# PSUM as two score strips and four single banks, with score pieces issued in twos

## The chip, the cores and the metric

The kernel runs on one core of one Trainium2 chip. The metric is the device time in microseconds (us); a median over several executions is quoted. The trace of one execution covers a span that is 1.6 to 1.9 us shorter than its time, so times are compared with times and spans with spans.

## The reference

Eight batches of eight-head causal attention (576 tokens, head size 64, and 16 "beacon" keys and values that every token may see), followed by an MLP with a squared ReLU over all 4608 tokens.

```python
B, H, S, Nb, D = (8, 8, 576, 16, 64)
k_all = np.concatenate([beacon_k, k], axis=2)
v_all = np.concatenate([beacon_v, v], axis=2)
scores = scale * np.matmul(q, k_all.transpose(0, 1, 3, 2))   # causal mask on the last S keys
a = np.exp(scores - scores.max(-1, keepdims=True))
a /= a.sum(-1, keepdims=True) + 1e-09
x = np.matmul(a, v_all)             # -> (4608, 512)
h = x @ w_in                        # 512 -> 2048
r = np.maximum(h, 0.0)
out = (r * r) @ w_out               # 2048 -> 512
```

## The kernel before

The kernel is not written in the order in which it runs. Every piece of work is an operation with modelled durations, a priority and the buffers it takes; a list scheduler plays these through and then emits the instructions of each engine in the order found. So a change of a buffer pool changes the order on all engines.

PSUM is where TensorE puts its results. The kernel takes it as eight banks of 512 fp32 columns. Before, these are four tiles of two banks each, shared by everything:

```python
ps = [psum.tile([128, 2, 512], FP32, name=f"ps{i}") for i in range(4)]
order = Order(
    pools={"ps": range(4), "stg": range(NSTG), "pt": range(NPT)},
    limits={"strip": 2, "av": 2, "mlp": 2, "tp": 1},
)
```

A head pair's scores come in four pieces. One piece fills one tile: the two heads of the pair are two 64-row matmuls, on the upper and the lower half of the array at once (their starts are 3 ns apart in the trace), each into its own bank. One exp on ScalarE (ACT) empties the tile.

```python
for i, (mms, off, width) in enumerate(ph.pieces):
    def emit_qk(e, mms=mms, box=box):
        st = ps[box["qk"].held[2]]
        for c, t0, t1, at in mms:
            for hj in range(2):
                hp = slice(64 * hj, 64 * hj + 64)
                nc.tensor.matmul(st[:, hj, at:at + t1 - t0],
                                 kT[b % 2][hp, pr, 128 * c:128 * c + 128],
                                 qT[b % 2][hp, pr, t0:t1], start=True, stop=True)
    qk = add(..., "PE", 0.05 + cols / 2400.0, emit_qk, ..., take=("ps", "strip"), gate=gate)
    # one exp for each piece; then a mask, AV (both heads in one tile), normalise
```

The MLP's units are two 128-column tiles of w_in for 512 tokens (eight 512-column matmuls, 1.73 us of TensorE), emptied by one relu over 1024 columns. The last output is copied and stored per 128 tokens, but both copies wait for the last matmul of both:

```python
deps = [s2_ops[j, u]]          # the last matmul unit of the two-tile output
ev = add(f"ev{j}.{u}", "ACT", 1.05 if ts is None else 0.6, emit_ev, prio=-15.0, deps=deps, ...)
```

For the first three batches q and k are transposed on TensorE (96x64 tiles; the beacon keys 16x128); later batches are transposed by DMA.

The softmax here doesn't subtract the row's maximum and nothing guards it: scores larger than these inputs give would overflow.

Of the kernel before, what the change touches and what calls it, by code (L numbers as in the profile page):

```python
# [9 lines left out]
FP32 = mybir.dt.float32  # L10
# [6 lines left out]
class Op:  # L17
# [3 lines left out]
                 "take", "give", "gate", "held", "dma", "pe_time", "behind", "followers",  # L21
                 "sync", "insts")

    def __init__(self, name, engs, dur, emit, prio=0.0, deps=(), take=None, give=None,
                 gate=None, dma=0.0, pe_time=0.0, behind=(), sync=()):
        self.name = name
        self.engs = engs if isinstance(engs, (tuple, list)) else (engs,)
        self.dur = dur
        self.emit = emit
        self.prio = prio  # L30
        self.sync = list(sync)
        self.need = list(deps) + self.sync
        self.users = []
        self.take = take
        self.give = give
        self.gate = gate
        self.held = None
        self.dma = dma
        self.pe_time = pe_time
        self.behind = list(behind)  # L40
        self.followers = []


class Order:
# [18 lines left out]
    def run(self):  # L63
# [24 lines left out]
        while events:  # L88
            now = events[0][0]
            while events and events[0][0] <= now + 1e-9:  # L90
# [6 lines left out]
                elif kind == "give":  # L97
                    pool, cls, idx = op.give.held
                    self.pools[pool].append(idx)
                    if cls in self.inuse:  # L100
                        self.inuse[cls] -= 1
            again = True
            while again:
                again = False
                for e in engines:
# [4 lines left out]
                    for op in avail[e]:  # L110
                        if any(free[x] <= now + 1e-9 for x in op.engs[:op.engs.index(e)]):
                            continue
                        if op.take:
                            pool, cls = op.take
                            if not self.pools[pool]:
                                continue
                            if cls in self.limits and self.inuse[cls] >= self.limits[cls]:
# [21 lines left out]
                    if op.take:  # L139
                        pool, cls = op.take  # L140
                        op.held = (pool, cls, self.pools[pool].pop(0))
                        if cls in self.inuse:
                            self.inuse[cls] += 1
# [33 lines left out]
def kernel(  # L177
# [62 lines left out]
    rcp = [sb(f"rcp{i}", [128, 2, NT], FP32) for i in range(4)]  # L240
    tri = sb("tri", [128, 4, 128], BF16)
    ps = [psum.tile([128, 2, 512], FP32, name=f"ps{i}") for i in range(4)]

    def wait_for(later, first):
# [4 lines left out]
        pools={"ps": range(4), "stg": range(NSTG), "pt": range(NPT)},  # L249
        limits={"strip": 2, "av": 2, "mlp": 2, "tp": 1},  # L250
# [126 lines left out]
    def add_strided(b, prio):  # L377
# [17 lines left out]
        for pr in range(HP):  # L395
# [3 lines left out]
            def emit_tp(e, pr=pr, h=h, box=box):  # L399
                pp = ps[box["t"].held[2]].bitcast(BF16)  # L400
                nc.tensor.transpose(pp[:, 1, 0:Nb], bks[b % 2][:, h, :], ident[0:Nb, 0:Nb])
                for half, at, t in ((1, Nb, ks), (0, 0, qs)):
                    for u in range(NS):
                        for hj in range(2):
                            nc.tensor.transpose(pp[64 * hj:64 * hj + 64, half, at + u * NP:at + (u + 1) * NP],  # L405
                                                t[b % 2][:, 2 * pr + hj, u, :], ident[0:NP, 0:NP])

            busy = qk_ops[HP * (b - 2) + pr] if b >= 2 else []
            tp = add(f"tp{b}.{pr}", "PE", 0.8 if b else 1.3, emit_tp, prio=100.0 * (HP * b + pr) - 190,
                     deps=[bk, loads[pr, "k"], loads[pr, "q"], ident_op] + busy, take=("ps", "tp"))  # L410
            box["t"] = tp

            def emit_k(e, pr=pr, box=box):
                pp = ps[box["t"].held[2]].bitcast(BF16)
                copy_on(e, kT[b % 2][:, pr, 0:Nb], pp[:, 1, 0:Nb])
                copy_on(e, kT[b % 2][:, pr, Nb:Nb + S].rearrange("p (n s) -> p n s", s=NS),
                        pp[:, 1, Nb:Nb + S].rearrange("p (s n) -> p n s", s=NS))

            def emit_q(e, pr=pr, box=box):
                pp = ps[box["t"].held[2]].bitcast(BF16)  # L420
                copy_on(e, qT[b % 2][:, pr, 0:S].rearrange("p (n s) -> p n s", s=NS),
                        pp[:, 0, 0:S].rearrange("p (s n) -> p n s", s=NS))

            ek = add(f"ek{b}.{pr}", "DVE", 0.9, emit_k, prio=-200.0, deps=[tp])
            eq = add(f"eq{b}.{pr}", ("DVE", "ACT"), 0.75, emit_q, prio=-199.0, deps=[tp])
            add(f"tpg{b}.{pr}", "-", 0.0, None, prio=0.0, deps=[ek, eq], give=tp)
# [67 lines left out]
    def add_phase(b, pr, p, n, ph, take_pt, qk_deps, gate):  # L494
        base = 100.0 * p + 1000.0 * n
        exps = []
        for i, (mms, off, width) in enumerate(ph.pieces):
            cols = sum(max(96, t1 - t0) for _, t0, t1, _ in mms)
            box = {}

            def emit_qk(e, mms=mms, box=box):
                st = ps[box["qk"].held[2]]
                for c, t0, t1, at in mms:
                    for hj in range(2):
                        hp = slice(64 * hj, 64 * hj + 64)
                        nc.tensor.matmul(  # L506
                            st[:, hj, at:at + t1 - t0],
                            kT[b % 2][hp, pr, 128 * c:128 * c + 128],
                            qT[b % 2][hp, pr, t0:t1],
                            start=True, stop=True,  # L510
                        )

            qk = add(f"qk{p}.{n}.{i}", "PE", 0.05 + cols / 2400.0, emit_qk, prio=base + i,
                     deps=qk_deps + [take_pt], take=("ps", "strip"), gate=gate)
# [3 lines left out]
            def emit_exp(e, off=off, width=width, box=box):  # L518
                st = ps[box["qk"].held[2]]
                nc.scalar.activation(pt[take_pt.held[2]][:, :, off:off + width], st[:, :, 0:width],  # L520
                                     AF.Exp, bias=0.0, scale=scale)

            exps.append(add(f"exp{p}.{n}.{i}", "ACT", 0.18 + 2 * width / 1200.0, emit_exp, prio=base + i,
                            deps=[qk], give=qk))
# [16 lines left out]
        def emit_av(e):  # L541
            P = pt[take_pt.held[2]]
            a = ps[av.held[2]]
            for hj in range(2):
                h = 2 * pr + hj
                for t in tl:
                    for c in range(t + 1):
# [3 lines left out]
                            a[:, hj, (t - tl[0]) * (D + 1):(t - tl[0] + 1) * (D + 1)],  # L551
# [5 lines left out]
        av = add(f"av{p}.{n}", "PE", 0.07 + 0.064 * sum(t + 1 for t in tl), emit_av, prio=base - 150,  # L557
                 deps=[mask] + [cast[b, "v", c] for c in range(tl[-1] + 1)] + av_ops[p], take=("ps", "av"),
                 give=take_pt if ph is phases(b)[-1] else None)
        av_ops[p].append(av)  # L560

        def emit_norm(e):
            a = ps[av.held[2]][:, :, 0:nt * (D + 1)].rearrange("p h (t d) -> p h t d", d=D + 1)
            r = rcp[(2 * p + n) % len(rcp)][:, :, 0:nt]
            nc.vector.reciprocal(r, a[:, :, :, D])  # L565
            nc.vector.tensor_tensor(  # L566
                out=xn[b % 2].rearrange("p t (h d) -> p h t d", d=D)[:, 2 * pr:2 * pr + 2, tl[0]:tl[0] + nt],
                in0=a[:, :, :, 0:D],
                in1=r[:, :, :, None].to_broadcast([128, 2, nt, D]),
                op=ALU.mult,  # L570
            )

        deps = [av]
        if b >= 2:
            deps += [o for (bb, _), o in xt_ops.items() if bb == b - 2]
        norm_ops[p, n] = add(f"norm{p}.{n}", "DVE", 0.4 + 0.133 * nt, emit_norm, prio=base - 150, deps=deps, give=av)
# [5 lines left out]
    s2_first = {}  # L582
# [7 lines left out]
    def add_xt(b):  # L590
        for t in range(NT):
# [7 lines left out]
            deps = [norm_ops[HP * b + i, 0] for i in range(HP)] + ring_deps(tok, tok + n)  # L599
# [4 lines left out]
    def add_xt_pe(b):  # L604
        for k, ph in enumerate(phases(b)):
            for pr in range(HP):
# [3 lines left out]
                def emit_tp(e, pr=pr, box=box, ph=ph):  # L610
                    pp = ps[box["t"].held[2]].bitcast(BF16)
                    for t in ph.tiles:
                        n = t_rows(t)
                        nc.tensor.transpose(pp[:, 0, t_start(t):t_start(t) + n],
# [3 lines left out]
                         deps=[norm_ops[HP * b + pr, k]], take=("ps", "tp"))  # L618
                box["t"] = tp

                def emit_ev(e, pr=pr, box=box, lo=lo, hi=hi):
                    pp = ps[box["t"].held[2]].bitcast(BF16)
                    at = (b * S) % RING
                    copy_on(e, xT[:, pr, at + lo:at + hi], pp[:, 0, lo:hi])
# [28 lines left out]
    def add_chunk(j):  # L653
# [11 lines left out]
        for f in range(NFT // 2):  # L665
            sqs = []
            for n, (lo_, hi_) in enumerate(parts):
                spans = [(lo_, wrap), (wrap, hi_)] if lo_ < wrap < hi_ else [(lo_, hi_)]
                N = hi_ - lo_
                box = {}  # L670

                def emit_s1(e, f=f, spans=spans, box=box):
                    h = ps[box["s1"].held[2]]
                    for u in range(2):
                        ft = 2 * f + u
                        for lo, hi in spans:
                            for mc in range(NMC):
                                nc.tensor.matmul(h[:, u, lo - spans[0][0]:hi - spans[0][0]],  # L678
# [4 lines left out]
                s1 = add(f"s1.{j}.{f}.{n}", "PE", 1.73 * N / TCH, emit_s1, prio=base + f + 0.5 * n,  # L683
                         deps=feeds_of(lo_, hi_) + [w_ops["in", f // 2]]
                         + [s2_ops[j - 2, u] for u in range(2) if j >= 2],
                         take=("ps", "mlp"), pe_time=1.73 * N / TCH)
                box["s1"] = s1
                s1_ops[lo_, hi_].append(s1)

                def emit_relu(e, f=f, lo=lo_ - t0, hi=hi_ - t0, box=box):  # L690
                    h = ps[box["s1"].held[2]][:, :, 0:hi - lo]
                    dst = G[:, 2 * f:2 * f + 2, lo:hi]
                    if e == "ACT":
                        nc.scalar.activation(dst, h, AF.Relu, bias=0.0, scale=1.0)  # L694
                    else:
# [138 lines left out]
```

## Time and profile before

| | before |
|---|---|
| time, median of 4 | 355.49 us (354.92 to 356.18) |
| span of the trace | 353.2 us |
| TensorE busy | 334.7 us (95%) |
| first matmul, first MLP matmul | 4.2 us, 27.6 us |
| start of the last matmul to the end | 5.1 us |

The head of the page, and its row of the granted clock:

```profile
span 353.2 us, 7173 instructions
...
PE 334.7 (95%) x2943; PEld 178.6 (51%) x2980; DVE 148.9 (42%) x287; ACT 193.4 (55%) x233; POOL 85.5 (24%) x132
...
PEclk9999999999999999999999999999999999999999
```

PE is TensorE and PEld its weight loads, DVE is VectorE, POOL GpSimd. 2943 matmuls are recorded and the program has 2980: 37 records are missing.

The row of the clock reads 9 (90% or more) from the start, and there it misleads: the trace has no record of the clock before 24.3 us, and until then TensorE runs at half pace. Two runs of the same 24 AV matmuls, one on each side:

```profile
22.60 1.52 PE L550 MATMUL ps<-vb,pt 128*128 128x65 bf16 x24
24.77 0.89 PE L550 MATMUL ps<-vb,pt 128*128 128x65 bf16 x24
```

From start to start the median AV matmul takes 54 ns before 24.3 us and 29 ns after it, a pair of transposes 80 and 43 ns.

Next, who TensorE waited for after 27 us, from the list of waits (total us, times, longest):

```profile
PE ps L506 <- DMA kT<-qk_area: 1.0, 1, 1.0
PE ps L678 <- ACT qT L280: 0.6, 1, 0.6
PE ps L718 <- issue: 0.5, 3, 0.2
PE ps L718 <- DMA stg<-in_k_dram: 0.2, 1, 0.2
```

So TensorE almost never waits after the start, and still "busy" is not "useful". The timeline of TensorE shows why (columns: start, length, engine, line, operation, output<-inputs, shapes, count). L506 are scores, L718 and L678 the MLP, L550 attention output (AV):

```profile
179.64 0.38 PE L506 MATMUL ps<-qT,kT 64*128 64x496 bf16 x2
179.95 1.68 PE L718 MATMUL ps<-w_out,g 128*128 128x512 bf16 x7
181.78 0.55 PE L506 MATMUL ps<-qT,kT 64*128 64x464 bf16 x6
182.26 1.90 PE L718 MATMUL ps<-w_out,g 128*128 128x512 bf16 x8
184.10 0.30 PE L506 MATMUL ps<-qT,kT 64*128 64x208 bf16 x4
184.33 1.90 PE L718 MATMUL ps<-w_out,g 128*128 128x512 bf16 x8
186.07 1.91 PE L678 MATMUL ps<-xT,w_in 128*128 128x256 bf16 x16
```

Read starts, not lengths (the ends of matmuls are modelled). Between two runs without a score run (184.33 to 186.07) eight 512-column matmuls take 1.74 us, or 216 ns each. From 182.26 to 184.10 the same eight take 1.84: about 0.10 us more, because a score run follows. The score run of 184.10 has 208 + 80 columns, 0.12 us at 2400 columns per us (256 columns take 109 ns from start to start, 512 take 216), and the next run starts 0.23 us later: another 0.11. A score run between full-array work thus costs about 207 ns beyond its columns, and the same for one piece (179.64, 184.10) as for two (181.78: 464 columns, then 336 and 80). The Trainium skill, "TensorEngine Tiling (Array Packing)", Key Properties, states that a change of tiling mode drains TensorE; this trace agrees in that each change costs time, and gives the size.

The end of the timeline (L280 copies of the output; "SPq" issues stores):

```profile
346.84 1.01 ACT L280 COPY osb<-ps 128x1024 f32<-128x1024 f32 x1 [11.11 <-PE ps L718]
347.88 0.37 SPq L750 DMA_DIRECT2D out_dram<-osb  x1
348.57 1.07 ACT L280 COPY osb<-ps 128x512 f32<-128x512 f32 x2 [0.71 <-PE ps L718]
349.18 0.85 SPq L752 DMA_DIRECT2D out_dram<-osb  x2
```

### The profile page before, as it was taken

How to read it: one execution, taken by the hardware profiler on the slowest of the kernel's cores; microseconds unless marked ns; L12 is line 12 of the kernel's file. 1: busy time of each engine (PE TensorE's matmuls, PEld its weight loads, DVE VectorE, ACT ScalarE, POOL GpSimd, SP SyncE). 2: the span in 40 equal slices, each digit the busy share in tenths (PEclk: the TensorE clock that was granted, in tenths of full speed). 3: DMA queues.
4: the chain of work that ended last, by engine and by line, in shares of the span. 5: the costliest groups of instructions: out<-in, count | busy, mean ns of one | idle time of the engine just before them, and what ended most of it. 6: DMA issues, size and time to landing. Idle time of an engine off the chain costs nothing.

```text
span 353.2 us, 7173 instructions
## 1 busy us (share of the span) xinstructions
PE 334.7 (95%) x2943; PEld 178.6 (51%) x2980; DVE 148.9 (42%) x287; ACT 193.4 (55%) x233; POOL 85.5 (24%) x132
## 2 busy tenths in 40 slices
PE   3789999999999989999999999999999999999994
PEld 2459665554545444444446874445454444444441
DVE  5576674349714455146622753247132302301300
ACT  2686786287555764665745663676634405505602
POOL 7273721209215504133501651000000000000000
PEclk9999999999999999999999999999999999999999
DMA  7999999965969999699989999440013103003003
GB/s 101 183 160 204 223 206 211 201 169 118 206 116 236 223 221 191 138 224 222 251 137 202 248 213 209 115 118 11 0 61 69 59 0 121 0 0 121 0 0 119
DMA packets 137008, 49.49 MB, mean 140 GB/s; under 512 B 123344, under 2 KB 132048, under 8 KB 136976
## 3 DMA queue, kind: packets, MB, share of 16 engines
q1 hardware_dynamic: 127472, 40.09, 53.4%
q0 software_dynamic: 9504, 8.95, 15.7%
q8 instruction: 23, 0.38, 0.5%
q14 instruction: 9, 0.07, 0.1%
HBM read 37.22 MB, written 9.44 MB: 132 GB/s over the span
## 4 chain that ended last, share of the span: by engine, by line
PE 74%; DMA 12%; SPq 5%; ACT 4%; DVE 2%; issue 2%; POOL 1%; ACTq 0%; DVEq 0%; POOLq 0%
PE ps L678 32%; PE ps L718 27%; PE ps L550 7%; PE ps L506 6%; DMA stg<-in_k_dram 4%; DMA stg<-in_v_dram 4%; SPq L597 3%; ACT pt L520 2%; DMA kT<-qk_area 2%; DMA stg<-in_q_dram 1%; SPq L327 1%; DVE kT L282 1%; DMA qk_area<-in_q_dram 1%; PE ps L405 1%; ACT qT L280 1%
## 5 line engine op out<-in xcount | busy, mean ns | idle before, releaser
L678 PE MATMUL ps<-xT,w_in 128*128 128x512 bf16 (+3 forms) x689 | 131.9, 340 | 1.6 <-ACT qT L280 0.6
L718 PE MATMUL ps<-w_out,g 128*128 128x512 bf16 x554 | 129.5, 380 | 1.4 <-issue 0.5
L520 ACT ACTIVATE pt<-ps 128x832 bf16<-128x832 f32 (+4 forms) x128 | 105.3, 865 | 40.7 <-PE ps L506 40.2
L678 PEld LDWEIGHTS <-w_in 128*128 128x128 bf16 x704 | 66.0, 98 | 57.6 <-issue 6.0
L694 ACT ACTIVATE g<-ps 128x1024 bf16<-128x1024 f32 (+2 forms) x65 | 61.8, 951 | 54.0 <-PE ps L678 53.8
L718 PEld LDWEIGHTS <-g 128*128 128x128 bf16 x576 | 53.0, 98 | 65.7 <-issue 5.8
L703 DVE TENSOR_TENSOR g<-g 128x1024 bf16<-128x1024 bf16 (+2 forms) x80 | 53.0, 664 | 77.5 <-ACT g L694 77.0
L530 DVE TENSOR_TENSOR pt<-pt,tri 128x1024 bf16<-128x1024 bf16 (+1 forms) x36 | 24.8, 692 | 50.1 <-ACT pt L520 48.6
L282 POOL CAST qk_area<-stg 128x512 bf16<-128x512 f32 (+2 forms) x50 | 34.6, 704 | 35.0 <-DMA stg<-in_k_dram 18.7
L282 POOL CAST vb<-stg 128x512 bf16<-128x512 f32 (+1 forms) x38 | 26.0, 695 | 69.6 <-DMA stg<-in_v_dram 59.1
L506 PE MATMUL ps<-qT,kT 64*128 64x80 bf16 (+6 forms) x400 | 39.1, 291 | 1.7 <-DMA kT<-qk_area 1.0
L280 ACT COPY osb<-ps 128x1024 f32<-128x1024 f32 (+1 forms) x19 | 18.3, 969 | 40.6 <-PE ps L718 40.3
L550 PEld LDWEIGHTS <-pt 128*128 128x128 bf16 (+1 forms) x960 | 34.5, 99 | 8.8 <-issue 2.5
L550 PE MATMUL ps<-vb,pt 128*128 128x65 bf16 (+1 forms) x960 | 36.5, 196 | 1.9 <-DVE pt L530 0.9
L566 DVE TENSOR_TENSOR xn<-ps,rcp 128x640 bf16<-128x640 f32 (+2 forms) x36 | 27.0, 750 | 1.7 <-DMA xT<-xn 0.4
L506 PEld LDWEIGHTS <-kT 64*128 64x128 bf16 x400 | 13.7, 97 | 24.2 <-issue 18.8
L565 DVE RECIPROCAL rcp<-ps 128x10 f32<-128x10 f32 (+2 forms) x36 | 7.6, 211 | 38.1 <-PE ps L550 36.2
L696 DVE TENSOR_SCALAR g<-ps 128x1024 bf16<-128x1024 f32 (+2 forms) x15 | 15.8, 1053 | 7.8 <-PE ps L678 7.0
L280 ACT COPY qT<-ps 128x576 bf16<-128x576 bf16 x12 | 7.7, 640 | 16.1 <-DVE kT L282 13.0
L282 DVE COPY kT<-ps 128x16 bf16<-128x16 bf16 (+1 forms) x24 | 9.9, 456 | 9.7 <-PE ps L405 7.5
L405 PE MATMUL ps<-ident,qk_area 96*64 96x96 bf16 x288 | 11.1, 233 | 2.9 <-DMA qk_area<-in_k_dram 1.8
L534 DVE TENSOR_TENSOR pt<-pt,tri 80x160 bf16<-80x160 bf16 x32 | 10.8, 339 | 0.0
(31 smaller groups left out, 57.1 us busy)
## 6 DMA issues: line engine op xcount, KB each, us to landing
out_dram<-osb SPq DMA_DIRECT2D x17, 512.0 KB, 3.5
stg<-in_v_dram SPq DMA_DIRECT2D x21, 256.0 KB, 5.1
stg<-in_q_dram SPq DMA_DIRECT2D x20, 256.0 KB, 4.8
stg<-in_k_dram SPq DMA_DIRECT2D x15, 256.0 KB, 5.1
w_in<-in_moe_w_in_dram POOLq DMA_DIRECT2D x4, 512.0 KB, 8.2
w_out<-in_moe_w_out_dram POOLq DMA_DIRECT2D x4, 512.0 KB, 10.6
stg<-in_v_dram SPq DMA_DIRECT2D x7, 224.0 KB, 4.7
qk_area<-in_k_dram POOLq DMA_DIRECT2D x4, 288.0 KB, 12.4
```

What stands on the lines that cost most here:

```text
L280: nc.scalar.copy(dst, src)
L282: eng[e].tensor_copy(dst, src)
L506: nc.tensor.matmul(st[:, hj, at:at + t1 - t0], kT[b % 2][hp, pr, 128 * c:128 * c + 128], qT[b % 2][hp, pr, t0:t1], start=True, stop=True,)
L520: nc.scalar.activation(pt[take_pt.held[2]][:, :, off:off + width], st[:, :, 0:width], AF.Exp, bias=0.0, scale=scale)
L530: nc.vector.tensor_tensor(out=d, in0=d, in1=tri[:, m0:m0 + m, :][:, None].to_broadcast([128, 2, m, 128]), op=ALU.min)
L550: nc.tensor.matmul(a[:, hj, (t - tl[0]) * (D + 1):(t - tl[0] + 1) * (D + 1)], P[0:rr, hj, o:o + 128], vb[b % 2][0:rr, c, h, :], start=(c = ...
L566: nc.vector.tensor_tensor(out=xn[b % 2].rearrange("p t (h d) -> p h t d", d=D)[:, 2 * pr:2 * pr + 2, tl[0]:tl[0] + nt], in0=a[:, :, :, 0:D ...
L678: nc.tensor.matmul(h[:, u, lo - spans[0][0]:hi - spans[0][0]], w_in_sb[:, mc, ft * 128:(ft + 1) * 128], xT[:, mc, lo % RING:lo % RING + hi ...
L694: nc.scalar.activation(dst, h, AF.Relu, bias=0.0, scale=1.0)
L696: nc.vector.tensor_scalar(out=dst, in0=h, scalar1=0.0, scalar2=None, op0=ALU.max)
L703: nc.vector.tensor_tensor(out=d, in0=d, in1=d, op=ALU.mult)
L718: nc.tensor.matmul(o[:, ts, :], G[:, fc, (2 * u + ts) * 128:(2 * u + ts + 1) * 128], w_out_sb[:, fc, :], start=(fc == 0), stop=(fc == NFT ...
```

## The change

The intent is to give scores their own two strips, so that two pieces can be issued back to back as one run, and to pay for the four banks this takes by cutting all other units to a single bank. From batch 1 on the four pieces of a pair become two runs. The diff, cut to its core (cuts are marked "..."; the scheduler learns to take several buffers at once and give them back singly):

```diff
-    ps = [psum.tile([128, 2, 512], FP32, name=f"ps{i}") for i in range(4)]
+    strips = [psum.tile([128, 2, 512], FP32, name=f"strip{i}") for i in range(2)]
+    ps = [psum.tile([128, 512], FP32, name=f"ps{i}") for i in range(4)]
...
-        pools={"ps": range(4), "stg": range(NSTG), "pt": range(NPT)},
-        limits={"strip": 2, "av": 2, "mlp": 2, "tp": 1},
+        pools={"strip": range(2), "ps": range(4), "stg": range(NSTG), "pt": range(NPT)},
+        limits={"av": 2, "tp": 2},
...
+            for n, x in enumerate("kq"):          # k and q transposed in separate units
+                box[x] = add(f"tp{b}.{pr}{x}", "PE", 0.65 if b else 0.9, ...,
+                             deps=[bk if x == "k" else None, loads[pr, x], ident_op] + busy, take=("ps", "tp"))
...
-        for i, (mms, off, width) in enumerate(ph.pieces):
+        size = 2 if b >= 1 else 1
+        for i in range(0, len(ph.pieces), size):
+            group = ph.pieces[i:i + size]
...
-            qk = add(f"qk{p}.{n}.{i}", "PE", 0.05 + cols / 2400.0, emit_qk, prio=base + i,
-                     deps=qk_deps + [take_pt], take=("ps", "strip"), gate=gate)
+            qk = add(f"qk{p}.{n}.{i}", "PE", 0.24 + cols / 2400.0, emit_qk, prio=base + i,
+                     deps=qk_deps + [take_pt], take=("strip", "strip", len(group)), gate=gate)
...
+        for hj in range(2):                       # AV and normalise: one head, one bank
...
+                for ft in (2 * f, 2 * f + 1):     # MLP, first half: one 128-column tile, one bank
...
+        for ts in range(TCH // 128):              # MLP, second half: one 128-token tile, one bank
...
+            evs.append(add(f"ev{j}.{ts}", ("ACT", "DVE"), {"ACT": 0.62, "DVE": 0.66}, emit_ev, ..., deps=deps,
+                           give=first["s2"]))
```

## The prediction

> **What bounds the kernel now.** TensorE. The page shows PE busy 334.7 of 353.2 us (95%), at full clock. Busy is not useful, so I took gaps between matmul starts from the trace: 512-column MLP matmuls follow each other at 216 ns, AV matmuls at 29 ns. What is lost:
> 1. Switches of array mode. Scores use 64-row tiles in pairs, MLP and AV the full array. A score run between full-array work costs about 207 ns beyond its columns, whether it holds one piece or two. The Trainium skill, "TensorEngine Tiling (Array Packing)", Key Properties, says that a change of tiling mode drains TensorE; this trace agrees. By the order of instructions there are 81 score runs and 12 transpose runs: some 19 us.
> 2. Real waits: about 10 us before 27.6 us, when the MLP starts (loads, exps); afterwards 0.7 us (at 45.0), 0.3 (71.8) and 1.0 (130.5, on k/q loads and transposes).
> 3. The tail: the last matmul ends near 348.5, then two 128x512 copies in a row (1.07 us) and a store, to 353.2.
>
> **What the change does.** PE's 2980 matmuls keep number and shape. Score runs fall from 81 to 68; q/k transpose runs rise from 12 to 17, since k and q are separate; switches of mode fall from 185 to 167. At about 103 ns each: -1.9 us, all on the critical path, which is PE.
> Evictions get smaller and more: relu 128x1024 takes 1.02 us on ACT, 128x512 about 0.6 (544 columns took 0.63), so ACT does 103 of 0.6 for 54 of 1.02, and 33 output copies of 0.59 for 17 of 1.01: about +9 us of ACT. DVE gains about 15 us (split reciprocal and normalise, 25 relus of about 0.7, six qT copies). At 55% and 42% busy this is off the path unless a bank comes free late.
> Slack for that, from PE's order with measured spacing: from batch 1 on a strip pair is mostly wanted again 2.8 us or more after its last write, against 0.25 + 1.00 + 0.95 us for two exps (a relu of 0.6 may stand between: tight). MLP banks are refilled after 2.6 us in the MLP-only end, against 1.4 before. I expect few new waits: +0.8 us.
> In the load queue the xT transposes move some 7 loads later and k/q loads earlier: the wait at 130.5 should shrink, an xT wait may appear. Net -0.7 us with the other two waits.
> Tail: the next to last tile's copy no longer waits for the last: -0.5 us.
> The start is bound by loads and exps: -0.3.
>
> **Sum.** 355.7 - 1.9 + 0.8 - 0.7 - 0.5 - 0.3 = 353.1 us, range 350.2 to 356.8. Chances: faster by over 2% 0.06, within 2% 0.89, slower by over 2% 0.05. Most score pieces were already issued in twos, so little of the drain cost goes.
>
> **What would show the steps.** PE busy falls by about 2 us; score runs still cost 207 ns each, but 13 fewer; PE waits after 28 us stay under 3 us; ACT busy about 200, DVE about 164; MLP and AV spacing unchanged; first MLP matmul at 26 to 28 us; end of last matmul to end of span shorter by 0.5 us.
>
> **What would make it wrong.** Queueing behind exps on ACT, so that a bank or strip pair repeatedly comes free late (28 pairs, 0.3 us each: 8 us); late xT behind loads; or the extra semaphore waits of half-sized units breaking the 216 ns spacing.

## The result, and the profile after

| | before | after |
|---|---|---|
| time, median of 4 | 355.49 us | 351.47 us (351.30 to 352.77) |
| span of the trace | 353.2 us | 349.6 us |
| TensorE busy | 334.7 us | 335.9 us |
| first MLP matmul | 27.6 us | 26.5 us |
| start of the last matmul to the end | 5.1 us | 4.1 us |

The ratio is 0.990, with a 95% interval of 0.9878 to 0.9922. (Ratios are the mean time of one kernel's runs over that of the other's of the same rounds, so not quite the ratio of the medians.) The change is 1% faster, clear of noise.

The head of the page, the waits of TensorE after 27 us, a stretch of its timeline (L515 scores, L727 and L692 MLP, L563 AV) and the end of the timeline, answering to those of before:

```profile
span 349.6 us, 7413 instructions
...
PE 335.9 (96%) x2980; PEld 179.5 (51%) x2980; DVE 167.9 (48%) x391; ACT 197.3 (56%) x298; POOL 82.8 (24%) x132
```

```profile
PE ps L412 <- DMA qk_area<-in_q_dram: 0.5, 1, 0.5
PE ps L563 <- POOL vb L286: 0.4, 2, 0.2
PE ps L412 <- DMA qk_area<-in_k_dram: 0.3, 1, 0.3
```

```profile
182.42 0.48 PE L515 MATMUL strip<-qT,kT 64*128 64x336 bf16 x8
182.83 3.63 PE L727 MATMUL ps<-w_out,g 128*128 128x512 bf16 x16
186.29 0.61 PE L563 MATMUL ps<-vb,pt 128*128 128x65 bf16 x15
186.84 0.58 PE L515 MATMUL strip<-qT,kT 64*128 64x496 bf16 x4
187.35 0.63 PE L563 MATMUL ps<-vb,pt 128*128 128x65 bf16 x15
```

```profile
344.21 0.58 ACT L284 COPY osb<-ps 128x512 f32<-128x512 f32 x1 [4.58 <-PE ps L727]
344.82 2.09 SPq L754 DMA_DIRECT2D out_dram<-osb  x2
345.95 0.58 ACT L284 COPY osb<-ps 128x512 f32<-128x512 f32 x1 [1.15 <-PE ps L727]
```

A score run now has two pieces (four or eight matmuls) and costs what it cost: from 186.84 to 187.35 is 0.51 us for 496 + 464 columns (0.40), so 0.11 on leaving; entering costs another 0.1. No wait for a strip or a bank shows at all (waits under 150 ns are not listed), and the waits that remain are for loads. Of the last copies one runs 1.7 us ahead of the other.

"TensorE busy" rose by 1.2 us while the kernel got 3.6 us shorter. The Trainium skill, "Trainium Kernel Development and Optimization", Best Practices, warns that matmul busy is no measure of the distance to the peak; here it is worse, since the trace before lacks 37 matmuls and the one after lacks none (37 gaps of some 53 ns, the step of 432 ns less a recorded length of 379, are an estimated 2.0 us). I therefore split the span by the starts of the matmuls: for each run of one kind of matmul, its count from the program, at the measured spacing at full clock (216 ns for 512 columns, about 29.5 for AV and 42 for a pair of transposes); 103 ns for each switch of array mode, half of the 207; the rest are waits.

| us, from the traces | before | after | difference |
|---|---|---|---|
| matmuls at their spacing | 307.5 | 307.5 | 0 |
| switches of mode: 185, 167 | 19.1 | 17.2 | -1.9 |
| waits after the first MLP matmul | 3.0 | 1.8 | -1.2 |
| waits, and half clock, between the first matmul and the first MLP matmul | 11.9 | 12.1 | +0.2 |
| last matmul's start to the end | 5.1 | 4.1 | -1.0 |
| rest: 4.2 us before the first matmul, and gaps under 150 ns | 6.6 | 6.9 | +0.3 |

The rows add up to the spans. The row of switches is a count times a price, and experiment 1 tests the price. Counted gap by gap, with the 37 missing matmuls filled in, the waits after the first MLP matmul are 2.6 and 1.8 us, so that row is good to some 0.4. Of the 11.9 and 12.1 us some 6.1 and 6.5 are no waits but the half clock (an estimate: so long would the work issued before 24.3 and 25.9 us take at the spacings above, and at half clock it takes as much again). What is left as waits there is 5.8 and 5.6.

### The profile page after: what moved, and what is told of

It is laid out like the page before. It is cut to its first block, busy times and chain, and to the rows that moved or that the text cites. A ratio compares the mean times of both kernels' runs of the same rounds, so it can differ in the third digit from the quotient of the medians. Undisturbed runs are those within 1.5% of the kernel's fastest.

```text
span 349.6 us, 7413 instructions
## 1 busy us (share of the span) xinstructions
PE 335.9 (96%) x2980; PEld 179.5 (51%) x2980; DVE 167.9 (48%) x391; ACT 197.3 (56%) x298; POOL 82.8 (24%) x132
## 4 chain that ended last, share of the span: by engine, by line
PE 86%; DMA 9%; POOL 1%; SPq 1%; issue 1%; ACT 0%; POOLq 0%; ACTq 0%
PE ps L727 36%; PE ps L692 34%; PE ps L563 8%; PE strip L515 7%; DMA stg<-in_v_dram 5%; DMA qk_area<-in_k_dram 4%; SPq L331 1%; DMA qk_area<-in_q_dram 1%; POOL w_in L653 1%; PE ps L412 1%; POOL vb L286 0%; PE ps L628 0%; ACT osb L284 0%; POOL qk_area L392 0%; PE ps L409 0%
## 5 line engine op out<-in xcount | busy, mean ns | idle before, releaser
L692 PE MATMUL ps<-xT,w_in 128*128 128x512 bf16 (+3 forms) x704 | 134.4, 340 | 0.0
L727 PE MATMUL ps<-w_out,g 128*128 128x512 bf16 x576 | 130.5, 379 | 0.0
L530 ACT ACTIVATE pt<-strip 128x832 bf16<-128x832 f32 (+4 forms) x128 | 104.3, 863 | 37.3 <-PE strip L515 36.9
L708 ACT ACTIVATE g<-ps 128x512 bf16<-128x512 f32 (+2 forms) x126 | 70.3, 558 | 40.9 <-PE ps L692 39.8
L692 PEld LDWEIGHTS <-w_in 128*128 128x128 bf16 x704 | 65.1, 98 | 53.9 <-issue 2.5
L727 PEld LDWEIGHTS <-g 128*128 128x128 bf16 x576 | 54.2, 98 | 63.3 <-issue 1.2
L284 ACT COPY osb<-ps 128x512 f32<-128x512 f32 x33 | 19.3, 585 | 57.8 <-PE ps L727 57.8
L563 PEld LDWEIGHTS <-pt 128*128 128x128 bf16 (+1 forms) x960 | 37.3, 99 | 17.0 <-issue 8.1
L563 PE MATMUL ps<-vb,pt 128*128 128x65 bf16 (+1 forms) x960 | 42.6, 197 | 0.7 <-POOL vb L286 0.4
L515 PE MATMUL strip<-qT,kT 64*128 64x80 bf16 (+7 forms) x400 | 37.2, 293 | 0.1
L580 DVE TENSOR_TENSOR xn<-ps,rcp 128x320 bf16<-128x320 f32 (+2 forms) x72 | 32.7, 454 | 2.6
L579 DVE RECIPROCAL rcp<-ps 128x5 f32<-128x5 f32 (+2 forms) x72 | 13.4, 186 | 39.7 <-PE ps L563 39.3
L710 DVE TENSOR_SCALAR g<-ps 128x512 bf16<-128x512 f32 (+2 forms) x34 | 21.0, 620 | 16.9 <-PE ps L692 16.0
L515 PEld LDWEIGHTS <-kT 64*128 64x128 bf16 x400 | 12.9, 97 | 16.7 <-issue 12.7
L412 PEld LDWEIGHTS <-qk_area 96*64 96x64 bf16 x288 | 8.9, 126 | 6.3 <-DMA qk_area<-in_k_dram 2.7
```

Source lines behind the costliest of these rows:

```text
L412: nc.tensor.transpose(pp[64 * hj:64 * hj + 64, at + u * NP:at + (u + 1) * NP], t[b % 2][:, 2 * pr + hj, u, :], ident[0:NP, 0:NP])
L515: nc.tensor.matmul(st[:, hj, at:at + t1 - t0], kT[b % 2][hp, pr, 128 * c:128 * c + 128], qT[b % 2][hp, pr, t0:t1], start=True, stop=True,)
L530: nc.scalar.activation(pt[take_pt.held[2]][:, :, off:off + width], st[:, :, 0:width], AF.Exp, bias=0.0, scale=scale)
L563: nc.tensor.matmul(a[:, (t - tl[0]) * (D + 1):(t - tl[0] + 1) * (D + 1)], P[0:rr, hj, o:o + 128], vb[b % 2][0:rr, c, h, :], start=(c == 0) ...
L580: nc.vector.tensor_tensor(out=xn[b % 2].rearrange("p t (h d) -> p t h d", d=D)[:, tl[0]:tl[0] + nt, h], in0=a[:, :, 0:D], in1=r[:, :, None ...
L692: nc.tensor.matmul(h[:, lo - spans[0][0]:hi - spans[0][0]], w_in_sb[:, mc, ft * 128:(ft + 1) * 128], xT[:, mc, lo % RING:lo % RING + hi - lo],
```

## The experiments

All runs gave the right result. "Theory D" says that the gain is the drains: fewer switches of array mode, each about 103 ns of TensorE. "Rival L" says that it is the layout, by shorter waits for banks.

### 1 and 2. The cost of a switch by itself

The changed kernel, with one tiny matmul between the two pieces of each of the 56 grouped runs; once over the full array, once over 64 rows (the mode of the scores). Everything else keeps its order.

```diff
                 for s, (mms, _, _) in enumerate(group):
                     st = strips[box["qk"].slots[s]]
+                    if s:   # dummy_full
+                        nc.tensor.matmul(st[:, 0, 0:16], ident, ident[:, 0:16], start=True, stop=True)
+                    if s:   # dummy_rows, in its place
+                        nc.tensor.matmul(st[:, 0, 0:16], ident[0:64], ident[0:64, 0:16], start=True, stop=True)
```

> The changed kernel, with one 16-column full-array matmul put between the two score pieces of each of the 56 grouped runs (it writes strip columns that the second piece overwrites, so the result stays right); the order of everything else is the same. Theory D (a change of array mode costs TensorE about 103 ns, and a run in and out about 207): 56 more pairs of switches, +11.6 us for them and +1 to 2 for the matmuls themselves, so 363 to 366 us, and the start of piece two after piece one moves by 200 ns or more. Rival L (the gain over the kernel before came from the banks, and the 207 ns are only pipeline latency that a following matmul hides): +1 to 3 us, under 355.

> Control for the run before: the same 56 extra 16-column matmuls, but with 64 rows, so in the score matmuls' own mode. Theory D: only their own time, 56 times 7 to 60 ns, so +0.4 to +3 us over the changed kernel (351.5), and 9 to 12 us under the full-array version. Rival L: the same time as the full-array version within 1 us.

Measured: 362.67 us (362.49 to 363.06) with the full-array matmul, 353.24 us (352.34 to 354.27) with the 64-row one; 351.47 without either. The timelines of TensorE, with the weight load of the tiny matmul, first of the full-array run, then of the 64-row run:

```profile
150.76 0.38 PE L517 MATMUL strip<-qT,kT 64*128 64x496 bf16 x2
151.07 0.10 PEld L513 LDWEIGHTS <-ident 128*128 128x128 bf16 x1 [0.22 <-issue]
151.07 0.18 PE L513 MATMUL strip<-ident 128*128 128x16 bf16 x1
151.19 0.37 PE L517 MATMUL strip<-qT,kT 64*128 64x464 bf16 x2
```

```profile
154.68 0.38 PE L517 MATMUL strip<-qT,kT 64*128 64x496 bf16 x2
154.69 0.10 PEld L513 LDWEIGHTS <-ident 64*128 64x128 bf16 x1
154.90 0.17 PE L513 MATMUL strip<-ident 64*128 64x16 bf16 x1
154.90 0.38 PE L517 MATMUL strip<-qT,kT 64*128 64x464 bf16 x2
```

The second piece starts 0.43 us after the first where the array has to change mode twice, and 0.22 us after it where it does not (496 columns alone are 0.207 us). 56 times 0.21 us is 11.8 us; the full-array kernel is 11.2 us over the changed kernel, and 9.4 us over its control. The control lost some of its lead: the spans of the two traces differ by 8.6 us, and the control's trace, taken in the slowest of its four runs, has 2.6 us more waits than the full-array run's (one of 1.6 us on xT at 153.7 us, 1.1 us more at the start, where the half clock lasts until 26.8 us and not 24.1). So a switch costs what the prediction read from the gaps, and it is not hidden. Rival L's claim that the 207 ns are mere pipeline latency, which a following matmul hides, falls.

Whether the array drains or only the next weights come late, these runs do not separate. In the 64-row run the weights of the tiny matmul are loaded 0.21 us ahead of it, while piece one runs; in the full-array run the load starts 4 ns ahead. The same holds in the changed kernel: at each of the 116 switches after 50 us the first weight load of the new mode starts 1 to 5 ns before its matmul, within the MLP's runs of 512 columns 213 to 218 ns before. A late load alone would hardly cost 103 ns, since in AV runs the loads lead by some 28 ns and the matmuls keep their pace.

### 3 and 4. The layout without the twos, the twos without the layout

```diff
-        size = 2 if b >= 1 else 1
+        size = 1                          # singles: the changed kernel, one piece at a time
```

```diff
+        size = 2 if b >= 1 else 1         # before_twos: the kernel before, pieces in twos ...
+            group = ph.pieces[i:i + size]
+            qk = add(..., take=("ps", "strip", len(group)), gate=gate)   # ... two of the four shared tiles at once
```

> The changed kernel with score pieces issued one by one everywhere: the new banks without the twos. Score runs 90 in place of 68 and switches of mode 207 in place of 167 (the kernel before: 81 and 185). Theory D: +40 switches at 103 ns are +4.1 us over the changed kernel, so about 355.6, the kernel before's time: the new banks alone are worth the tail (-1.0) and lose it to 22 more switches (+2.3) than before. Rival L: within 1 us of the changed kernel, 351 to 352.5.

> The kernel before with its four shared two-bank tiles, only the score pieces issued in twos from batch 1 (two tiles taken at once). Score runs 65, switches 155 in place of 185. Theory D: -30 switches at 103 ns are -3.1 us, so 352.4 if no new wait appears. Rival L: taking two of the four shared tiles at once starves the MLP and the attention output, so waits on TensorE grow by several us and the time is 355.5 or more.

| | old tiles | new banks |
|---|---|---|
| pieces one by one | 355.23 (the kernel before, same rounds) | 359.67 (358.73 to 361.53) |
| pieces in twos | 370.82 (370.06 to 371.19) | 351.47 (the change) |

Both halves alone are slower: singles by 1.3% (ratio 1.0131, interval 1.0109 to 1.0152), before_twos by 4.4% (1.0435, 1.0421 to 1.0448). Theory D had 355.6 and 352.4, so it missed both; Rival L missed the first and had the second right in direction. The split of the spans says what happened: the switches went as D counted them (207 in singles, 21.3 us; 155 in before_twos, 16.0 us), and waits came on top. After the first MLP matmul they are 5.4 us in singles and 23.2 us in before_twos, against 1.8 in the changed kernel. The lists of TensorE's waits after 27 us, singles first, then before_twos (L557 is AV, L621 the transposes of attention output, L685 and L692 the MLP's first half):

```profile
PE ps L692 <- DMA xT<-xn: 2.4, 1, 2.4
PE ps L563 <- POOL vb L286: 1.4, 2, 0.8
...
```

```profile
PE ps L685 <- DMA xT<-xn: 8.1, 2, 4.1
PE ps L557 <- DVE pt L537: 2.0, 2, 1.7
PE ps L685 <- ACT pt L527: 1.5, 1, 1.5
PE ps L621 <- DVE xn L573: 1.2, 1, 1.2
...
```

The whole list of before_twos is 14.7 us. Some 3.0 of it are for a tile that ACT has still to empty; the largest part, 8.1, is for the transposed attention output (xT). The list is less than 23.2 us, because TensorE also lost clock. The page's row of the granted clock of before_twos, then its timeline around the wait at 119.5 us:

```profile
PEclk9999999959999699999999899999999999999999
```

```profile
123.68 0.59 PE L685 MATMUL ps<-xT,w_in 128*128 128x512 bf16 x1 [4.12 <-DMA xT<-xn]
...
124.48 1.91 PE L685 MATMUL ps<-xT,w_in 128*128 128x512 bf16 x4 [0.22 <-issue]
```

After a gap of 4.1 us four 512-column matmuls take 1.91 us, some 430 ns from start to start, twice the usual 216. The table by stretches gives a mean granted clock of 0.83 from 120 to 140 us and 0.80 from 60 to 80. The Trainium skill, "TensorE: Matmul & The Clock Gate", Part 1, has TensorE at half rate after an idle window of about 3.4 us. The half rate shows here; an idle window does not always. The clock fell at 72.0, 119.8 and 201.7 us (for 10.2, 6.8 and 3.4 us), and in the 3.4 us before TensorE was busy for 2.4, 1.5 and 0 us. The fall at 119.8 comes at the beginning of the 4.1 us gap, not after it.

### 5. Which part of the layout carries the twos

The kernel before with twos, where two of the four two-bank tiles are kept for scores and the other two serve everything else.

```diff
-        pools={"ps": range(4), ...
+        pools={"strip": range(2), "ps": range(2, 4), ...
-            take=("ps", "strip", len(group))
+            take=("strip", "strip", len(group))
```

> As before_twos (score pieces in twos on the old two-bank tiles), but two of the four tiles are reserved for scores and the other two serve the MLP, attention output and transposes. If dedicated strips alone make the twos affordable, the waits of before_twos shrink and the time is 352 to 356. If the single banks are what is needed (two two-bank tiles are too few for everything else), it is slower than before_twos' 370.8.

Measured: 366.91 us (365.87 to 368.23), ratio 1.0328 (1.0304 to 1.0353). Neither expectation holds. Dedicated strips take away 4 us, and 17.2 us of waits remain after the first MLP matmul, the longest again on xT:

```profile
PE ps L685 <- DMA xT<-xn: 5.8, 1, 5.8
```

What the changed kernel has beyond this one, with the same strips and the same twos, are single-bank units for the rest (and what comes with them: the split of k from q and of the output copies, new modelled durations, and no limit on MLP units in flight): with them the waits are 1.8 us. So most of the benefit of the layout lies in that part. That it is because four units, not two, can be in flight beside the scores is likely, but not shown: no run changes that alone.

### 6. The tail

```diff
-                deps = [s2_ops[j, u]]
+                deps = [s2_ops[j, u] if ts is None else s2_ts[j, u, ts]]   # the last matmul of this tile
```

> The kernel before, only its last two-tile output: the copy of the first tile waits for the first tile's matmuls, not for both. If the tail of the change (last matmul to end, 5.1 us before and 4.1 after) comes from that, -1.0 us: 354.4, with 4.1 us from the last matmul's start to the end, and nothing else changed.

Measured: 354.29 us (353.73 to 354.75), against 355.12 for the kernel before in the same rounds; ratio 0.9972 (0.9957 to 0.9987). The end of its timeline:

```profile
348.07 0.59 ACT L280 COPY osb<-ps 128x512 f32<-128x512 f32 x1 [0.71 <-PE ps L719]
348.69 0.35 SPq L754 DMA_DIRECT2D out_dram<-osb  x1
```

From the last matmul's start to the end are 4.4 us, where the kernel before has 5.1 and the changed one 4.1. So 0.7 of the 1.0 us come from this one dependency: one copy less in a row (0.5 us), and one store less behind it. What is left, 0.3 us, fits the two-tile store of 512 KB that this kernel, like the one before, issues 1.3 us before its last one; in the changed kernel the store ahead of the last is of 256 KB. That was not tested.

### 7 to 9. Taking out more switches

The change itself added five transpose runs by splitting k from q. "joined_tp" puts them back into one unit that takes two single banks. "joined_pad" also pads the beacon keys from 16 to 96 rows of zeros, so that their transposes have the same array shape as those after them. "best1" moves one memset of that padding behind the first cast.

```diff
-            for n, x in enumerate("kq"):
-                box[x] = add(f"tp{b}.{pr}{x}", "PE", 0.65 if b else 0.9, lambda e, x=x, f=emit_tp: f(e, x), ...,
-                             take=("ps", "tp"))
+            tp = add(f"tp{b}.{pr}", "PE", 1.3 if b else 1.8, lambda e, f=emit_tp: (f(e, "k"), f(e, "q")), ...,
+                     take=("ps", "tp", 2))                                     # joined_tp
...
-    bks = [sb(f"bks{i}", [Nb, H, D], BF16) for i in range(2)]
+    bks = [sb(f"bks{i}", [NP, H, D], BF16) for i in range(2)]                  # joined_pad, best1; set to 0 once
...
-                    nc.tensor.transpose(pp[:, 0:Nb], bks[b % 2][:, h, :], ident[0:Nb, 0:Nb])
+                    for hj in range(2):
+                        nc.tensor.transpose(pp[64 * hj:64 * hj + 64, 0:NP],
+                                            bks[b % 2][:, 2 * pr + hj, :], ident[0:NP, 0:NP])
```

> The changed kernel, with the transposes of k and q of a pair issued as one unit again (two single banks taken at once). Transpose runs 12 in place of 17, score runs 65 in place of 68, switches 158 in place of 167. Theory D: 9 fewer switches are -0.9 us, 350.5 if the start doesn't wait longer, since q now holds back k; rival: splitting k from q hides load time at the start, so joining costs 0.5 to 2 us, 352 to 353.5.

> As joined_tp, and the beacon keys' transposes (16 rows by 128 columns, an array shape of their own) are padded with zero rows to 96 by 64, the shape of the transposes that follow them. Twelve switches go: 146 in place of 158. Theory D: -1.2 us from joined_tp, so 349.3 us, less 24 matmuls of some 20 ns. Rival (only the scores' switches drain the array): no change from joined_tp.

> joined_pad with the memset of the zero rows moved: in joined_pad the two memsets (0.55 us on DVE) stood before the first beacon cast and pushed TensorE's first matmul from 4.20 to 4.87 us, which hid what the padding saved. Here one of them (0.27 us) stands before it and the other after. Theory D: 13 fewer switches than joined_tp are -1.3 us, +0.4 for the padded matmuls and at most +0.3 at the start: 348.9 us (joined_tp 349.7). Rival (the beacon transposes' switches cost nothing, or the start is bound by the loads): 349.5 to 349.9.

| | switches | time, median (range) | ratio to before (interval) | span |
|---|---|---|---|---|
| the change | 167 | 351.47 (351.30 to 352.77) | 0.990 (0.9878 to 0.9922) | 349.6 |
| joined_tp | 158 | 349.71 (348.66 to 349.89) | 0.9833 (0.9813 to 0.9852) | 348.0 |
| joined_pad | 145 | 349.46 (348.35 to 349.98) | 0.9832 (0.9813 to 0.9851) | 348.0 |
| best1 | 145 | 348.99 (348.67 to 349.72) | 0.9824 (0.9808 to 0.9840) | 347.3 |

(The expectations said 146; one more switch went, between two transposes.) joined_tp gained 1.8 us where D had 0.9: nine switches are 0.9, and in its trace the waits after the first MLP matmul are also 0.7 us shorter. The rival, that splitting k from q hides load time, does not show: the first MLP matmul starts at 26.2 us, against 26.5.

In joined_pad the switch itself goes: the median step from a beacon transpose to the next transpose is 64 ns in place of 108. The time did not follow, and the timeline says why for half of it: the first matmul starts at 4.87 us, not 4.20, since the zeroing stands in front of the first cast on VectorE. best1 has it at 4.45, and its span is 0.7 us under joined_tp's. In time the three overlap in range, so what the padding is worth, up to about 0.7 us, is not settled. best1 is the fastest kernel: 1.8% under the kernel before and 0.7% under the change by the medians.

### 10. Twos in the first batch too

```diff
-        size = 2 if b >= 1 else 1
+        size = 2                          # on best1
```

> best1 with score pieces in twos in batch 0 as well: switches 142 in place of 146. Theory D: up to -0.4 us; but the start waits on loads and exps, not on TensorE (about 12 us of waits before the first MLP matmul), so the saving should vanish in waits there: within 0.5 us of best1, or up to 1 us slower, since a pair of strips must be free at once.

Measured: 352.48 us (352.03 to 353.85), ratio 0.9925 (0.9907 to 0.9943); 3.5 us slower than best1, more than either side had. Four switches went, and the waits grew from 12.0 to 13.4 us before the first MLP matmul (half clock included) and from 1.0 to 3.4 us after it. Among TensorE's waits are, in best2:

```profile
PE strip L520 <- DVE kT L287: 1.2, 1, 1.2
...
PE strip L520 <- ACT pt L535: 0.7, 2, 0.5
```

And in best1:

```profile
PE strip L520 <- ACT pt L535: 1.3, 1, 1.3
```

It is tempting to say that asking for two strips at once makes scores later, but the waits for a strip (ACT pt, the exp that empties it) are 0.7 us here and 1.3 in best1. What the traces do show is that the half clock of the start lasts until 28.0 us, against 25.2, which is worth some 1.0 us by the estimate used above. The cause of the rest is open. The change was right to start with batch 1.

## Why the prediction was right

The range (350.2 to 356.8 us) held the measured 351.47, and "within 2%" was the likely class. The range also held the kernel before's own 355.49, so the terms say more than the range. The forecast difference was -2.6 us and the measured one -4.0 (-3.6 in the spans). Term by term:

- **Switches, -1.9 us: right.** 18 fewer as counted, and the price per switch held up when 112 were put in (experiment 1). That most pieces already went in twos, and so little was to be had, was right too: the program before has 81 score runs for 128 pieces.
- **The step that failed, "I expect few new waits: +0.8 us" with "Net -0.7 us with the other two waits".** Measured net -1.2 us (-0.8 counted gap by gap), where the sum had +0.1. The feared queueing of exps and relus on ACT never came: TensorE waits for no strip and no bank after 27 us. All three old waits are gone, and what is new (0.4 us at 33.6, 0.7 at 38.3, 0.7 at 45.0) are waits for q, k and v of batch 1, because TensorE comes to them earlier than the loads do (the first AV run of batch 1 starts at 43.8 us, against 47.7 before).
- **The tail, -0.5 us: the mechanism was right, the size was half.** It counted the copy that no longer stands in a row (0.5 us) and left out the second store behind it. Measured -1.0; the single dependency brings 0.7 of it (experiment 6).
- **The start, -0.3 us:** the row before the first MLP matmul went from 11.9 to 12.1 us, but some 0.4 of that is the half clock that lasted longer; the waits alone fell by about 0.2 (both by the estimate above). The prediction took TensorE to be "at full clock" throughout, which holds only after 24.3 us. The first MLP matmul starts 1.1 us earlier only because some AV work now comes after it.
- **"PE busy falls by about 2 us": wrong.** It rose by 1.2; with the estimated 2.0 us for the missing records put back it fell by some 0.8. ACT (197, forecast 200) and DVE (168, forecast 164) came out near; the spacing of MLP and AV matmuls is unchanged.
- What the prediction did not see is how much the two parts need each other. By its own price list, the layout alone would have been about neutral and the twos alone about -3 us; in fact they are +4 and +16.

What stays open: whether the waits of before_twos come from the shortage of tiles itself or from an order that the scheduler laid out with modelled durations and that the chip then did not keep. Both act together there, and no run separates them. All variants with twos, and singles too, also carry the new modelled duration of a score run (0.24 us beyond its columns in place of 0.05), which alone could change the order; no run tests that. Nor did any run isolate what removed the old waits (the row of -1.2 us).

## What to carry to other kernels

Count how often TensorE changes its array shape and read the price from the starts of the matmuls, not from the busy share; work of one shape should be issued together, and small transposes may be padded into the shape of their neighbours (worth at most some 0.7 us here, and not settled). Grouping needs buffers for the whole group at once. Here it paid only together with buffers of its own and halved units for all other work; either half of the change alone was a loss. Grouping in the first batch too was slower. Check the clock at the start by the steps of the matmuls, for the page's row read 9 where the trace had no record.

## What the Trainium skill lacked or had wrong

- "TensorEngine Tiling (Array Packing)" says that a change of mode drains TensorE but gives no size: here 207 ns for a run in and out (0.43 against 0.22 us between two pieces in experiments 1 and 2), whatever the run's length.
- The same page speaks of tiling for packing; it does not say that a single transpose of 16 rows between others of 96x64 also pays for a mode of its own: the step to the next transpose was 108 ns, and 64 ns when padded to the same shape.
- "TensorE: Matmul & The Clock Gate", Back-to-back issue gap, gives about 131 ns per 512-column matmul for a stream of weight loads and matmuls. Both traces show 216 ns throughout such streams, which is the figure that it gives for isolated ones.
- "TensorE: Matmul & The Clock Gate", Part 1, ties the half rate to an idle window of about 3.4 us: before_twos fell to half rate after 3.4 us with 2.4 and with 1.5 us of TensorE work in them.
- No page says that matmul records can be missing from a trace (37 of 2980 before, none after), which turned the sign of the difference in "TensorE busy".
